# One resource for two engines in a planner, K of two heads in one load, a new order for the shared query tile, and norm rows in spare bank columns

## The chip, the cores and the metric

The kernel runs on one core of a Trainium2 chip. The metric is device time in microseconds. The kernel before took 733.95 us, the median of 3 runs (733.51 to 734.59). The execution that was profiled took 733.62 us, and its trace has a span of 731.5 us, so 2.1 us lie outside the span.

## The reference

Three blocks follow one another. Attention over 2 batches and 8 heads has pooled queries: neighbouring queries are averaged, so that 1152 keys meet 576 queries in each head. An MLP with softplus takes 512 features to 2048 and back. An RMS norm and a gated MLP with SiLU (512 to 1536 and back) end the work.

```python
# q, k, v: (2, 8, 1152, 64)
q_pool = q.reshape(B, H, S // 2, 2, D).mean(axis=3)
scores = scale * np.matmul(q_pool, k.transpose(0, 1, 3, 2))
scores = scores - np.max(scores, axis=-1, keepdims=True)
attn = np.exp(scores)
attn = attn / (np.sum(attn, axis=-1, keepdims=True) + 1e-09)
x = (attn @ v) reshaped to (1152, 512)
h = x @ w_in                                   # 512 -> 2048
g = np.maximum(h, 0.0) + np.log1p(np.exp(-np.abs(h)))
x = g @ w_out                                  # 2048 -> 512
rms = np.sqrt(np.mean(x * x, axis=-1, keepdims=True) + 1e-06)
xn = x / rms * rms_g
g = xn @ w_gate                                # 512 -> 1536
val = xn @ w_val
out = (g * sigmoid(g) * val) @ w_out           # 1536 -> 512
```

## The kernel before

**Numbers in two halves.** A float32 operand is kept as a high half, which the matmul format holds exactly, and a low half, the rest. A product is three matmuls: high by high, low by high, high by low (`terms`, L517 to L519). So each operand costs a cast (high) and a subtraction (low): `kk` for the keys, `qh` and `ql` for the queries, `gh` and `gl` for the hidden layer, `x` for the MLP inputs, `w` for the weights. The weights come packed and are first decoded by four operations (L296 on ACT, L301, L304 and L306 on DVE).

**Attention** goes over 8 pairs of heads. `prep` (L330) loads K, Q and V of a pair, adds neighbouring queries (`qs`), and makes the halves. `qk` (L378) makes a tile's scores for 128 queries of a head against all 1152 keys, in three banks `s`. `softmax` takes the maximum (`nm`, DVE, L407) and the exponential (`p`, ACT, L409). `flip` (L417) transposes `p` through two banks `t` and copies it to `pt`. `av` (L436) multiplies by V into a bank `t`, and a copy takes it to `O`. Each head has 4 whole query tiles; the two half tiles that are left are merged into a fifth, x = NF, the shared tile. There `scales` (L453) makes the factors of the row sums: `den` (L457), a reciprocal (L459), and two spreading copies `rdb` (L460, L463). The transposes of the shared tile are groups T[0], T[1], T[2] (`flip_m`, L655).

**The two MLPs** go over three blocks of 384 tokens. For each block, `project` makes hidden columns in the banks `s`, a softplus or SiLU on ACT follows (`g`, L539 or L630), `halve` makes `gh` and `gl`, and the second matrix accumulates in other banks. Between the MLPs, `norm_sum`, `norm_rows` (L582) and `norm` (L603) make the RMS norm of a block while the next block is projected. The sums of squares are turned into rows in a bank of the ring `banks["h"]`, the ring that `project` uses, read by DVE (L590), and the factors are transposed in that same bank and copied to `rs`.

**What sets the order.** All operations are recorded in a `Plan`. Its `run()` is a list scheduler: each operation has one or several engines with a cost each (`dve`, `act`, `pool`, L188 to L197) and a latest start; the operation that can start first goes first, ties by latest start. If another engine than the quickest is nearly as soon (within SLACK), it is preferred: POOL first, then ACT. The matmuls keep their recorded order. The instructions are then emitted by planned start, and on the chip each engine works through its own queue in that order.

**Names in the rows.** L248 is the helper `tt` (subtractions and sums on DVE or POOL), L243 is a copy or cast on ACT, L245 one on DVE, and L251 is a load. Buffer numbers after a name, as in `kk_2124`, tell pairs and rounds apart.

Of the kernel before, what the change touches and what calls it, by code (L numbers as in the profile page):

```python
# [12 lines left out]
F32 = mybir.dt.float32  # L13
# [48 lines left out]
class Plan:  # L62
# [40 lines left out]
    def order(self):  # L103
# [27 lines left out]
        for o in reversed(topo):  # L131
            e, d = o.opts[0]
# [12 lines left out]
    def run(self):  # L145
        free = dict.fromkeys(("PE", "ACT", "DVE", "POOL", "SP", "NONE"), 0.0)
# [7 lines left out]
        while ready:  # L154
            starts = [(max(free[e], o.ready), o, e, d) for o in ready for e, d in o.opts]
            low = min(x[0] for x in starts)
            t, o, e, d = min((x for x in starts if x[0] <= low + 1e-9), key=lambda x: (x[1].late, x[0] + x[3], x[1].n))
            found = [(t, e, d)]
            for x in starts:
                if x[1] is o and x[2] != e and not any(  # L160
                        y[2] == x[2] and y[1].late < o.late and y[0] < x[0] + x[3] for y in starts):
                    found.append((x[0], x[2], x[3]))
            t, e, d = min(found, key=lambda x: x[0] + x[2])
            for want in ("POOL", "ACT"):
                for t2, e2, d2 in found:
# [22 lines left out]
def dve(n, fast=False):  # L188
    return "DVE", 0.157 + n / (1920 if fast else 960)
# [11 lines left out]
def body(ctx: ExitStack, tc: tile.TileContext, kT, qT, v, w1, w1o, wg, wv, w2o, rg, outT):  # L201
# [48 lines left out]
    def load(out, src, kb, w):  # L250
        return op([("SP", 0.07 + kb / 220)], lambda e: nc.sync.dma_start(out=out(), in_=src), w=w, lat=2.2)  # L251
# [31 lines left out]
    def decode(n):  # L283
# [17 lines left out]
        op([("DVE", 0.6)], lambda e: nc.vector.tensor_scalar(out=t1(), in0=word(0), scalar1=29, scalar2=None,  # L301
# [28 lines left out]
    def prep(pb):  # L330
# [3 lines left out]
        s["q"] = qx[pb % 2]  # L334
        for h in range(2):
            spare = pb == 0 and h == 1
            qr = ring("a", "p1", [P, 2, SQ], F32, 2) if spare else ring("e", "qr", [P, 2, SQ])
            for z in range(2):
                load(lambda qr=qr, z=z: qr()[z * D:z * D + D], qT[n + h], 288, [(qr, z)])
            kr = ring("a", "p0", [P, S], F32, 2) if spare else ring("e", "kr", [P, S])  # L340
            for z in range(2):
                load(lambda kr=kr, z=z: kr()[z * D:z * D + D], kT[n + h], 288, [(kr, z)])
            qs = ring("e", "qs", [P, SQ])
            qh, ql = s["q"][h]
            op([pool(SQ)] if pb else [dve(SQ)], lambda e, qs=qs, qr=qr: tt(e, qs(), qr()[:, 0, :], qr()[:, 1, :], ALU.add),
# [3 lines left out]
            for x, m, src in ((0, f, 0), (c, D, f)):  # L349
# [51 lines left out]
    def softmax(pb, x, h):  # L401
# [5 lines left out]
        op([dve(S)], lambda e: nc.vector.tensor_reduce(out=nm(), in_=sc()[:, :, :N], axis=AX.XY, op=ALU.max, negate=True),  # L407
# [9 lines left out]
    def flip(pb, x, todo):  # L417
# [14 lines left out]
        op([act(n * P, False), dve(n * P)],  # L432
# [3 lines left out]
    def av(pb, x):  # L436
# [14 lines left out]
        op([dve(n), act(n, False)], lambda e: copy(e, o()[:, x * P:x * P + n], t()[:, :n]), r=[(t, None)], w=[(o, x)])  # L451

    def scales(pb):  # L453
# [353 lines left out]
```

## Time and profile before

| | |
|---|---|
| median of 3 runs | 733.95 us (733.51 to 734.59) |
| profiled execution | 733.62 us, its span 731.5 us |
| PE busy | 688.9 us, 94% of the span |
| DVE busy | 472.0 us, 65% |
| ACT busy | 305.7 us, 42% |
| POOL busy | 176.6 us, 24% |
| HBM read and written | 59.25 MB and 2.36 MB |

PE is the TensorE matmul queue, DVE the vector engine, ACT the scalar engine, POOL the GpSimd engine, SP the engine that issues most loads. A row of instructions gives start, duration, engine, line, operation, the tile written and the tile read. What stands in brackets is the time for which the engine sat idle before it, and what ended that idle time. The granted clock (PEclk) is a share of TensorE's full speed. In the 40 slices of the span, PE is below nine tenths in the first slice, in three others (at 8) and in the last (at 7).

### The profile page before, as it was taken

How to read it: one execution, taken by the hardware profiler on the slowest of the kernel's cores; microseconds unless marked ns; L12 is line 12 of the kernel's file. 1: busy time of each engine (PE TensorE's matmuls, PEld its weight loads, DVE VectorE, ACT ScalarE, POOL GpSimd, SP SyncE). 2: the span in 40 equal slices, each digit the busy share in tenths (PEclk: the TensorE clock that was granted, in tenths of full speed). 3: DMA queues.
4: the chain of work that ended last, by engine and by line, in shares of the span. 5: the costliest groups of instructions: out<-in, count | busy, mean ns of one | idle time of the engine just before them, and what ended most of it. 6: DMA issues, size and time to landing. Idle time of an engine off the chain costs nothing.

```text
span 731.5 us, 12416 instructions
## 1 busy us (share of the span) xinstructions
PE 688.9 (94%) x5083; PEld 660.4 (90%) x5083; DVE 472.0 (65%) x761; ACT 305.7 (42%) x549; POOL 176.6 (24%) x129
## 2 busy tenths in 40 slices
PE   2999999999989999999999999889999999999997
PEld 2889898888989889998999999879999999999997
DVE  5788988989886678997325368997974242222222
ACT  1766677777667674443211243434432111010001
POOL 0441634444330112320013134563440020000000
PEclk9999999999999999999999999989999999999999
DMA  9575538274410013444000014333440100000001
GB/s 218 141 187 132 151 94 208 76 187 112 138 42 26 1 59 116 161 157 143 1 1 1 30 58 144 129 132 115 151 138 30 43 1 1 1 26 19 0 1 44
DMA packets 19145, 62.41 MB, mean 85 GB/s; under 512 B 2704, under 2 KB 4240, under 8 KB 19088
## 3 DMA queue, kind: packets, MB, share of 16 engines
q1 hardware_dynamic: 18944, 61.61, 29.2%
q8 instruction: 40, 0.66, 0.4%
q14 instruction: 17, 0.14, 0.1%
q10 hardware_dynamic: 144, 0.00, 0.0%
HBM read 59.25 MB, written 2.36 MB: 84 GB/s over the span
## 4 chain that ended last, share of the span: by engine, by line
PE 72%; DVE 21%; issue 3%; ACT 2%; DMA 1%; SPq 0%; POOL 0%; DVEq 0%; ACTq 0%
PE s L517 11%; PE s L518 11%; PE s L519 11%; PE s L391 10%; PE t L446 9%; PE t L428 8%; PE t L517 4%; PE t L519 4%; PE t L518 4%; DVE t L306 3%; DVE t L304 3%; DVE nm L407 2%; DVE t L301 2%; DVE den L457 2%; DVE gh L245 1%
## 5 line engine op out<-in xcount | busy, mean ns | idle before, releaser
L517 PE MATMUL s<-x,w 128*128 128x384 f32 x348 | 118.5, 341 | 7.3 <-ACT g L539 3.0
L519 PE MATMUL s<-x,w 128*128 128x384 f32 x348 | 117.2, 337 | 0.0
L518 PE MATMUL s<-x,w 128*128 128x384 f32 x348 | 117.0, 336 | 0.0
L407 DVE TENSOR_REDUCE nm<-s 128x1 f32<-128x1152 f32 x72 | 97.0, 1354 | 27.9 <-PE s L391 24.9
L248 POOL TENSOR_TENSOR w<-t,w 128x512 fp32r<-128x512 f32 x54 | 75.6, 1402 | 144.9 <-ACT w L243 119.2
L409 ACT ACTIVATE p<-s,nm 128x1152 f32<-128x1152 f32 x72 | 88.1, 1223 | 20.5 <-DVE nm L407 18.7
L243 ACT COPY pt<-t 128x512 f32<-128x512 f32 (+1 forms) x130 | 68.5, 536 | 61.8 <-PE t L428 46.1
L428 PE MATMUL t<-ident,p 128*128 128x128 f32 x576 | 83.3, 278 | 9.2 <-DVE O L245 7.9
L517 PE MATMUL s<-gh,w 128*128 128x384 f32 x243 | 82.6, 340 | 2.7 <-DVE gh L245 2.7
L428 PEld LDWEIGHTS t<-ident,p 128*128 128x128 f32 x576 | 65.9, 141 | 19.2 <-ACT p L409 10.2
L518 PE MATMUL s<-gl,w 128*128 128x384 f32 x243 | 82.5, 339 | 0.6 <-DVE gl L248 0.6
L519 PE MATMUL s<-gh,w 128*128 128x384 f32 x243 | 82.2, 338 | 0.0
L446 PE MATMUL t<-pt,v 128*64 128x128 f32 (+1 forms) x1440 | 80.1, 265 | 2.1 <-ACT pt L243 2.1
L630 ACT ACTIVATE g<-s 128x384 f32<-128x384 f32 x36 | 17.7, 491 | 150.0 <-PE s L519 150.0
L446 PEld LDWEIGHTS t<-pt,v 128*64 128x64 f32 x1440 | 71.3, 137 | 9.3 <-issue 5.2
L517 PEld LDWEIGHTS s<-x,w 128*128 128x128 f32 x348 | 65.5, 188 | 10.0 <-ACT g L539 4.3
L245 DVE CAST gh<-g 128x384 fp32r<-128x384 f32 x75 | 36.3, 484 | 46.2 <-PE t L519 44.1
L518 PEld LDWEIGHTS s<-x,w 128*128 128x128 f32 x348 | 65.7, 189 | 0.0
L519 PEld LDWEIGHTS s<-x,w 128*128 128x128 f32 x348 | 65.6, 189 | 0.0
L296 ACT ACTIVATE t<-raw 128x512 f32<-128x512 f32 x68 | 45.7, 673 | 41.2 <-POOL w L248 24.8
L248 POOL TENSOR_TENSOR kk<-kr,kk 64x1152 fp32r<-64x1152 f32 x14 | 38.0, 2715 | 89.7 <-DVE kk L245 44.4
L306 DVE SCALAR_TENSOR_TENSOR t<-t,t 128x512 int32<-128x512 int32 x68 | 54.5, 801 | 3.6 <-ACT t L296 1.6
(135 smaller groups left out, 1211.1 us busy)
## 6 DMA issues: line engine op xcount, KB each, us to landing
kr<-in_kT_dram SPq DMA_DIRECT2D x30, 288.0 KB, 4.7
qr<-in_qT_dram SPq DMA_DIRECT2D x30, 288.0 KB, 6.1
raw<-in_w_dram SPq DMA_DIRECT2D x16, 512.0 KB, 3.7
raw<-in_w1o_dram SPq DMA_DIRECT2D x16, 512.0 KB, 3.6
raw<-in_wg_dram SPq DMA_DIRECT2D x12, 512.0 KB, 3.4
raw<-in_wv_dram SPq DMA_DIRECT2D x12, 512.0 KB, 3.4
raw<-in_w2o_dram SPq DMA_DIRECT2D x12, 512.0 KB, 3.4
v<-in_v_dram SPq DMA_DIRECT2D x16, 288.0 KB, 3.2
```

Source lines behind the costliest of these rows:

```text
L243: nc.scalar.copy(out, in_)
L248: engines[e].tensor_tensor(out=out, in0=in0, in1=in1, op=o)
L296: o = op([("ACT", 0.68)], lambda e: nc.scalar.activation(out=t0(), in_=word(1).bitcast(F32), scale=2.0 ** -112, **(dict(func=AF.Prelu, alp ...
L306: op([dve(DM)], lambda e: nc.vector.scalar_tensor_tensor(out=t0().bitcast(I32), in0=t0().bitcast(I32), scalar=3, in1=t1(), op0=ALU.logical ...
L391: nc.tensor.matmul(sc()[:, c, :N], lhsT=q, rhs=s["kk"][hh]()[:, c * N:(c + 1) * N], start=(hh == heads[0] and z == 0), stop=(hh == heads[- ...
L407: op([dve(S)], lambda e: nc.vector.tensor_reduce(out=nm(), in_=sc()[:, :, :N], axis=AX.XY, op=ALU.max, negate=True), r=[(sc, None)], w=[(n ...
L409: o = op([("ACT", 1.42)], lambda e: nc.scalar.activation(out=pr(), in_=sc()[:, :, :N], func=AF.Exp, bias=nm(), accum_out=s["den"]()[:, col ...
L428: nc.tensor.transpose(t()[:, i * P:(i + 1) * P], pr[:, c * P:(c + 1) * P], ident)
L446: nc.tensor.matmul(t()[h * D:h * D + D, :n], lhsT=s["v"][h]()[:, c, :], rhs=rhs, start=(c == 0), stop=(c == CK - 1))
L517: nc.tensor.matmul(out, lhsT=w[:, 0, cols], rhs=hi, start=start, stop=False)
L518: nc.tensor.matmul(out, lhsT=w[:, 0, cols], rhs=lo, start=False, stop=False)
L519: nc.tensor.matmul(out, lhsT=w[:, 1, cols], rhs=hi, start=False, stop=stop)
```

## The change

The change has four parts.

1. **Planner.** Every POOL operation, and every DVE operation that touches no PSUM bank, now also takes a common resource, "PORT": two of these never overlap in the plan. DVE operations that read PSUM are marked `psum=True` and stay free of it. POOL is not preferred any more; ACT still is, over DVE. A load costs the plan at least 0.6 us. The sums `qs` and the subtractions for `kk` may go to DVE or POOL.
2. **K of two heads in one load.** K of a pair is loaded once, as 128 partitions (64 for each head), where before each head's K was loaded twice into 64 partitions. Its high half is cast in place, its low half is written to the other 64 partitions. The Q loads of the first pair are issued from ACT's queue instead of SP's.
3. **Shared tile.** Its order was: scores of the next pair's first tile, T[0], T[1], `av` of the tile before, T[2]. Now it is T[0], T[1], the scores, T[2], `av`.
4. **Norm rows.** They are made in columns 384 to 511 of the three banks of the first ring entry, which `project` doesn't use, instead of in a bank of the ring.

The core of the diff:

```diff
-            starts = [(max(free[e], o.ready), o, e, d) for o in ready for e, d in o.opts]
+            starts = []
+            for o in ready:
+                for e, d, *port in o.opts:
+                    t = max(free[e], o.ready)
+                    if port or e == "POOL":
+                        t = max(t, free["PORT"])
+                    starts.append((t, o, e, d, bool(port) or e == "POOL"))
...
-            t, e, d = min(found, key=lambda x: x[0] + x[2])
-            for want in ("POOL", "ACT"):
-                for t2, e2, d2 in found:
-                    if e2 == want and e not in ("POOL", want) and t2 < t + SLACK and t2 + d2 + SLACK < o.late + self.span:
-                        t, e, d = t2, e2, d2
+            t, e, d, port = min(found, key=lambda x: x[0] + x[2])
+            for x in found:
+                if x[1] == "ACT" and e == "DVE" and x[0] < t + SLACK and x[0] + x[2] + SLACK < o.late + self.span:
+                    t, e, d, port = x
...
             free[e] = t + d
+            if port:
+                free["PORT"] = t + d
...
-def dve(n, fast=False):
-    return "DVE", 0.157 + n / (1920 if fast else 960)
+def dve(n, fast=False, psum=False):
+    t = 0.157 + n / (1920 if fast else 960)
+    return ("DVE", t) if psum else ("DVE", t, 1)
...
+        kr = ring("e", "kr", [P, S])
+        load(kr, kT[n:n + 2].rearrange("a d s -> (a d) s"), 576, [(kr, None)])
...
-                load(lambda qr=qr, z=z: qr()[z * D:z * D + D], qT[n + h], 288, [(qr, z)])
-            kr = ring("a", "p0", [P, S], F32, 2) if spare else ring("e", "kr", [P, S])
-            for z in range(2):
-                load(lambda kr=kr, z=z: kr()[z * D:z * D + D], kT[n + h], 288, [(kr, z)])
+                load(lambda qr=qr, z=z: qr()[z * D:z * D + D], qT[n + h], 288, [(qr, z)], "ACTQ" if pb == 0 else "SP")
...
-            op([pool(SQ)] if pb else [dve(SQ)], lambda e, qs=qs, qr=qr: tt(e, qs(), qr()[:, 0, :], qr()[:, 1, :], ALU.add),
+            op([dve(SQ), pool(SQ)], lambda e, qs=qs, qr=qr: tt(e, qs(), qr()[:, 0, :], qr()[:, 1, :], ALU.add),
...
+            hi, lo = slice(h * D, h * D + D), slice(D - h * D, P - h * D)
+            op([act(S)] if pb == 0 else [dve(S, True), act(S)], lambda e, kk=kk, hi=hi: copy(e, kk()[hi], kr()[hi]),
+               r=[(kr, None)], w=[(kk, 0)])
+            op([dve(S), pool(S)], lambda e, kk=kk, hi=hi, lo=lo: tt(e, kk()[lo], kr()[hi], kk()[hi], ALU.subtract),
+               r=[(kr, None), (kk, 0)], w=[(kk, 1)])
...
-    def norm_rows(t, acc, bank):
-        b, m, view = bank
+    def norm_rows(t, acc):
+        b, m, view = spare(0)
...
+    def spare(m):
+        sx = banks["h"][0][0]
+        if m == 0 and "spare" not in banks:
+            banks["spare"] = [plan.buf(lambda: sx()[:, :, N:]) for _ in range(2)]
+        return banks["spare"][m], None, lambda: sx()[:, m, N:]
...
                 scales(pb)
+                T[0]()
+                T[1]()
                 if not last:
                     qk(pb + 1, 0, 0)
-                T[0]()
-                if last:
+                else:
                     make_banks(1, "h")
                     m1_h(0)
-                T[1]()
+                T[2]()
                 av(*prev)
-                T[2]()
```

The planner's new resource changes which engine takes what. From before to after, the instructions on POOL that subtract `w` go from 54 to 21 (on DVE from 11 to 44), those that subtract `gl` from 9 to 0 (on DVE from 75 to 84), and those that make `x` of 384 columns from 20 to 12 (8 more on DVE). Casts go from DVE to ACT: `kk`, 15 on DVE to 5 and 1 on ACT to 11; `qh` of 512 columns, 15 to 2 and 1 to 14; `gh`, 75 to 66 and 9 to 18; `w`, 18 to 9 and 47 to 56.

DVE's queue at the first pair, before: `kk` is K in halves, `qs` the summed queries, `p_110` and `p_116` a lent buffer with K and Q of the second head, `nm` the maximum of the first scores.

```order
L245 CAST kk_108<-kr 128x1152
L248 TENSOR_TENSOR kk_108<-kr,kk_108 64x1152
L248 TENSOR_TENSOR qs<-qr 128x576
L374 TENSOR_SCALAR qhA_88<-qs 128x512
L355 SCALAR_TENSOR_TENSOR qlA_90<-qs,qhA_88 128x512
L355 SCALAR_TENSOR_TENSOR qlA_90<-qs,qhA_88 128x64
L245 CAST kk_130<-p_110 128x1152
L248 TENSOR_TENSOR kk_130<-p_110,kk_130 64x1152
L407 TENSOR_REDUCE nm_137<-s 128x1
L248 TENSOR_TENSOR qs<-p_116 128x576
L374 TENSOR_SCALAR qhB_92<-qs 128x512
L355 SCALAR_TENSOR_TENSOR qlB_94<-qs,qhB_92 128x512
```

The same stretch of DVE's queue after:

```order
L256 TENSOR_TENSOR qs<-qr 128x576
L383 TENSOR_SCALAR qhA_90<-qs 128x512
L363 SCALAR_TENSOR_TENSOR qlA_92<-qs,qhA_90 128x512
L256 TENSOR_TENSOR kk_114<-kr,kk_114 64x1152
L363 SCALAR_TENSOR_TENSOR qlA_92<-qs,qhA_90 128x64
L256 TENSOR_TENSOR qs<-p_107 128x576
L256 TENSOR_TENSOR kk_121<-kr,kk_121 64x1152
L416 TENSOR_REDUCE nm_142<-s 128x1
L363 SCALAR_TENSOR_TENSOR qlB_96<-qs,qhB_94 128x512
```

The casts of `kk` have left DVE for ACT, and the first subtraction of `kk` now stands behind the queries' halves.

DVE's queue where the fifth pair ends and the sixth begins, before (the shared tile's `den` and `rdb`, then the two first maxima of the next pair):

```order
L245 CAST kk_2124<-kr 128x1152
L374 TENSOR_SCALAR qhA_88<-qs 128x64
L355 SCALAR_TENSOR_TENSOR qlA_90<-qs,qhA_88 128x64
L245 COPY O<-t 128x128
L457 TENSOR_SCALAR den<-den 128x9
L459 RECIPROCAL den<-den 128x9
L245 COPY pt<-t 128x4x128
L460 COPY rdb<-den 128x512
L407 TENSOR_REDUCE nm_2169<-s 128x1
L407 TENSOR_REDUCE nm_2181<-s 128x1
L463 COPY rdb<-den 128x128
```

The same place after:

```order
L253 CAST kk_2067<-kr 64x1152
L363 SCALAR_TENSOR_TENSOR qlA_92<-qs,qhA_90 128x64
L253 COPY O<-t 128x128
L466 TENSOR_SCALAR den<-den 128x9
L468 RECIPROCAL den<-den 128x9
L469 COPY rdb<-den 128x512
L416 TENSOR_REDUCE nm_2110<-s 128x1
L416 TENSOR_REDUCE nm_2134<-s 128x1
L472 COPY rdb<-den 128x128
```

The row `L245 COPY pt` has left the place between the reciprocal and `rdb`; the rest stands as before.

POOL's queue at that place, before:

```order
L248 TENSOR_TENSOR x_765<-y,x_765 128x384
L248 TENSOR_TENSOR x_770<-y,x_770 128x192
L248 TENSOR_TENSOR kk_2124<-kr,kk_2124 64x1152
L248 TENSOR_TENSOR qs<-qr 128x576
L248 TENSOR_TENSOR w_2157<-t_2062,w_2157 128x512
```

And after:

```order
L256 TENSOR_TENSOR x_759<-y,x_759 128x384
L256 TENSOR_TENSOR x_761<-y,x_761 128x192
L256 TENSOR_TENSOR qs<-qr 128x576
L256 TENSOR_TENSOR kk_2067<-kr,kk_2067 64x1152
L256 TENSOR_TENSOR kk_2161<-kr,kk_2161 64x1152
L256 TENSOR_TENSOR w_2179<-t_1827,w_2179 128x512
```

The sum `qs` now stands ahead of `kk`, and two subtractions of `kk` stand together.

## Rows read from the trace of the kernel before

**Rows 1.** The page: busy time of each engine.

```profile
PE 688.9 (94%) x5083; PEld 660.4 (90%) x5083; DVE 472.0 (65%) x761; ACT 305.7 (42%) x549; POOL 176.6 (24%) x129
```

**Rows 2.** PE's groups by line and shape: busy, mean ns, idle before, releasers.

```profile
L517 PE MATMUL s<-x,w 128*128 128x384 f32 x348 | 118.5, 341 | 7.3 <-ACT g L539 3.0 <-DVE n L590 2.6 <-ACT g L630 0.6
...
L428 PE MATMUL t<-ident,p 128*128 128x128 f32 x576 | 83.3, 278 | 9.2 <-DVE O L245 7.9 <-ACT p L409 0.9 <-ACT pt L243 0.2
L517 PE MATMUL s<-gh,w 128*128 128x384 f32 x243 | 82.6, 340 | 2.7 <-DVE gh L245 2.7
L518 PE MATMUL s<-gl,w 128*128 128x384 f32 x243 | 82.5, 339 | 0.6 <-DVE gl L248 0.6
...
L517 PE MATMUL t<-x,w 128*128 128x384 f32 x108 | 36.8, 340 | 2.0 <-ACT rs L243 1.3 <-DVE rs L245 0.7
```

**Rows 3.** Stretches of the span: busy time and count by engine, granted clock, DMA, GB/s.

```profile
84.00:240.00 156.00, 149.23 (x1567) 135.44 (x1566) 127.11 (x192) 111.44 (x195) 56.60 (x36) 1.00 0.42 111
430.00:490.00 60.00, 53.50 (x297) 51.74 (x296) 55.50 (x75) 26.42 (x48) 32.29 (x24) 0.97 0.38 126
486.80:493.30 6.50, 5.87 (x17) 5.47 (x18) 6.38 (x8) 2.85 (x4) 3.65 (x3) 0.50 0.45 153
541.00:544.50 3.50, 3.50 (x13) 3.49 (x12) 1.74 (x2) 1.10 (x3) 2.41 (x3) 0.51 0.75 240
600.00:640.00 40.00, 40.00 (x232) 40.00 (x232) 8.84 (x18) 2.95 (x6) 0.00 (x0) 1.00 0.00 1
```

**Rows 4.** The timeline, DVE at the longest wait of the decode stage.

```profile
485.35 1.44 DVE L245 CAST gh<-g 128x384 fp32r<-128x384 f32 x1
```

**Rows 5.** The timeline where the fifth pair of heads ends.

```profile
172.53 2.66 POOL L248 TENSOR_TENSOR kk<-kr,kk 64x1152 fp32r<-64x1152 f32 x1 [6.71 <-DVE qhA L374]
...
173.05 2.18 DVE L457 TENSOR_SCALAR den<-den 128x9 f32<-128x9 f32 x1
...
175.27 1.42 POOL L248 TENSOR_TENSOR qs<-qr 128x576 f32<-128x576 f32 x1
...
175.94 1.04 DVE L460 COPY rdb<-den 128x512 f32<-128x512 f32 x1
...
176.90 2.61 DVE L407 TENSOR_REDUCE nm<-s 128x1 f32<-128x1152 f32 x2
...
177.46 2.19 PE L446 MATMUL t<-pt,v 128*64 128x128 f32 x36 [0.29 <-ACT pt L243]
...
179.54 1.22 ACT L409 ACTIVATE p<-s,nm 128x1152 f32<-128x1152 f32 x1
...
181.15 0.63 PE L428 MATMUL t<-ident,p 128*128 128x128 f32 x4 [1.24 <-DVE O L245]
```

**Rows 6.** One tile's instructions, `den`: durations least, median and most, in ns.

```profile
L457 DVE TENSOR_SCALAR den<-den x8: 173/2174/2304, 41.7 to 270.9; 128x9 f32<-128x9 f32 x8
...
L460 DVE COPY rdb<-den x8: 416/1038/1466, 44.7 to 274.0; 128x512 f32<-128x512 f32 x8
```

**Rows 7.** The timeline where the sixth pair ends, PE.

```profile
214.30 0.63 PE L428 MATMUL t<-ident,p 128*128 128x128 f32 x4 [1.70 <-DVE O L245]
```

**Rows 8.** The timeline of the start.

```profile
8.43 0.76 DVE L248 TENSOR_TENSOR qs<-qr 128x576 f32<-128x576 f32 x1 [0.42 <-DMA qr<-in_qT_dram]
...
16.95 1.16 PE L391 MATMUL s<-kk,qlB 128*128 128x384 f32 x3
```

**Rows 9.** Two stretches of the start, columns as above.

```profile
2.00:6.00 4.00, 0.00 (x0) 0.00 (x0) 0.20 (x2) 0.01 (x1) 0.00 (x0) 1.00 1.02 237
12.00:15.80 3.80, 0.00 (x0) 0.00 (x0) 3.67 (x4) 1.24 (x3) 0.00 (x0) 1.00 1.06 287
```

**Rows 10.** Groups of DVE and ACT by line and shape: prices.

```profile
L248 DVE TENSOR_TENSOR w<-t,w 128x512 fp32r<-128x512 f32 x11 | 7.5, 686 | 0.3 <-ACT w L243 0.2
```

**Rows 11.** The same view for ACT.

```profile
L243 ACT CAST w<-t 128x512 fp32r<-128x512 f32 x47 | 29.0, 621 | 29.1 <-DVE t L306 27.6 <-PE t L518 1.4
...
L243 ACT CAST kk<-kr 128x1152 fp32r<-128x1152 f32 x1 | 1.1, 1141 | 0.0
```

More of the change, by code (lines that the diff above doesn't have):

```diff
@@ L131, in order @@
         for o in reversed(topo):
-            e, d = o.opts[0]
+            e, d = o.opts[0][:2]
             need = 0.0
@@ L145, in run @@
     def run(self):
-        free = dict.fromkeys(("PE", "ACT", "DVE", "POOL", "SP", "NONE"), 0.0)
+        free = dict.fromkeys(("PE", "ACT", "DVE", "POOL", "SP", "ACTQ", "PORT", "NONE"), 0.0)
         self.free = free
@@ L154, in run @@
         while ready:
-            starts = [(max(free[e], o.ready), o, e, d) for o in ready for e, d in o.opts]
+            starts = []
[5 more added lines that the diff above has]
+                    starts.append((t, o, e, d, bool(port) or e == "POOL"))
             low = min(x[0] for x in starts)
-            t, o, e, d = min((x for x in starts if x[0] <= low + 1e-9), key=lambda x: (x[1].late, x[0] + x[3], x[1].n))
-            found = [(t, e, d)]
+            t, o, e, d, port = min((x for x in starts if x[0] <= low + 1e-9), key=lambda x: (x[1].late, x[0] + x[3], x[1].n))
+            found = [(t, e, d, port)]
             for x in starts:
@@ L171, in run @@
                 fits = [x for x in starts if x[2] == e and x[0] + x[3] <= u[0] + 1e-9 and len(x[1].opts) == 1]
-                t, o, e, d = min(fits, key=lambda x: (x[0], x[1].late, x[1].n)) if fits else u
+                t, o, e, d, port = min(fits, key=lambda x: (x[0], x[1].late, x[1].n)) if fits else u
             ready.remove(o)
@@ L248, in tt, with load @@
         engines[e].tensor_tensor(out=out, in0=in0, in1=in1, op=o)
-    def load(out, src, kb, w):
-        return op([("SP", 0.07 + kb / 220)], lambda e: nc.sync.dma_start(out=out(), in_=src), w=w, lat=2.2)
+    def load(out, src, kb, w, queue="SP"):
+        q = nc.sync if queue == "SP" else nc.scalar
+        return op([(queue, 0.6 + max(0, kb / 220 - 0.6))], lambda e: q.dma_start(out=out(), in_=src), w=w, lat=2.2)
     xs = [fixed("k", f"x{t}", [P, 2 * KC * N], F32R) for t in range(NBLK)]
@@ L456, in scales @@
         rd = s["rd"] = ring("a", "rdb", [P, NF + 1, 2, D])
-        op([("DVE", 0.17)], lambda e: nc.vector.tensor_scalar(out=den(), in0=den(), scalar1=1e-9, scalar2=None, op0=ALU.add),
+        op([("DVE", 0.17, 1)], lambda e: nc.vector.tensor_scalar(out=den(), in0=den(), scalar1=1e-9, scalar2=None, op0=ALU.add),
            w=[(den, None)])
-        op([("DVE", 0.25)], lambda e: nc.vector.reciprocal(den(), den()), w=[(den, None)])
+        op([("DVE", 0.25, 1)], lambda e: nc.vector.reciprocal(den(), den()), w=[(den, None)])
         op([dve(NF * P)], lambda e: nc.vector.tensor_copy(
```

54 lines of the change are left out of this document (26 added, 28 removed).

## The prediction

> **What bounds the kernel now.** I read the page's busy times first, then PE's groups by line, then single stretches and the timeline at PE's longest waits. PE is busy for 688.9 of 731.5 us [rows 1], so what can be won lies in its waits and in stretches at a low clock. PE's groups name the waits [rows 2]: at the pair boundaries the transposes wait 7.9 us for DVE's copy of `O`; the projections wait 3.0 for ACT's softplus `g` and 2.6 for the norm's DVE row L590; the second matrices of the MLP wait 2.0 for `rs`; and the hidden layer's products wait 2.7 for `gh` and 0.6 for `gl`. Two stretches hold a granted clock near one half, so the lower level of 1.2 GHz: 486.8 to 493.3 and 541.0 to 544.5 [rows 3]. The first stands right behind the 2.7 us wait for `gh` (one wait: the group's only one), the second behind a wait of the norm. In attention DVE works 127 of 156 us and ACT 111 [rows 3]; in the decode stage DVE works 55.5 of 60 us, which is why the `gh` wait exists.
>
> DVE is slower than it needs to be. `den`, 9 columns, takes 0.17 us at best and 2.17 in the median; `rdb` takes 0.42 at best and 1.04 in the median [rows 6]. The long ones lie under a POOL instruction: `den` starts at 173.05 while POOL works on `kk` from 172.53 to 175.19, and ends 0.04 us behind it; `rdb` starts at 175.94 under POOL's `qs` [rows 5]. A cast of `gh` takes 1.44 us in the decode stage [rows 4]. In the same stretch at the boundary the maxima, which read PSUM, run at 1.31 us each, under POOL work or not. This is what the planner's new resource describes.
>
> **The change part by part**, against the profiled 733.62 us; that lies 0.33 below the median of 733.95, within the runs' spread.
>
> *Norm rows.* The next projection no longer shares a bank with the norm's rows and transposes, so its waits for L590 and, through the same ring, those of the second matrix for `rs` have no cause left: 2.6 + 2.0 = −4.6. What comes next in PE's queue has its operands long before, since the projection reads `x` and weights only. A new wait could be that the next norm's rows wait for the `rs` copy of the last one, but that lies a whole block back. With the wait before 541 gone, I take its low clock to go too. A steady stretch has 232 matmuls in 40.0 us, 0.172 each; the 13 of the slow stretch would take 2.24 in place of 3.50 [rows 3]: −1.3.
>
> *Planner, decode stage.* 33 subtractions of `w`, 9 of `gl` and 8 of `x` move from POOL to DVE. On DVE one of `w` costs 0.69 [rows 10], so 33 × 0.69 = 23 us of DVE work are added over the whole kernel; against that nothing holds DVE up where POOL is empty, and 9 casts of `gh` and 9 of `w` leave for ACT, which has room (26 of 60 us busy [rows 3]). Which of the two sums is larger can't be read off the order. A `gh` that costs 1.44 where nothing else but a cast of 384 columns is done shows a DVE that loses about 1 us each time; from the busy stretch I take it that the queue gets shorter. Then the waits for `gh` and `gl` go, 2.7 + 0.6 = −3.3, and the clock stays up behind them: 17 matmuls, 5.87 us busy, at 0.172 would take 2.93: −2.9. Of ACT's `g` waits I take half, 3.0 / 2 = −1.5, since ACT gets 18 more casts there at about 0.6 [rows 11] and loses waits on DVE. Bounds for this part: nothing gained (0) to all of it gained (−9.2, with the whole 3.0); I take −7.7.
>
> *Shared tile and POOL's order at the boundary.* The transposes of the next tile don't wait for the copy of `O` any more, as `av` is recorded behind T[2]. What is late next is ACT's exponential. PE's flip at 181.15 needs the exponential that starts at 179.54 and takes 1.22 [rows 5], so it ends at 180.76, and some 0.2 later with its sum: hardly before the flip started. And the chain ahead of it moves. POOL now has `qs`, then `kk`, back to back: 1.42 + 2.66 = 4.08 us. If the first starts about where POOL's `kk` starts before, 172.5 to 172.8, that is up to 174.2 and on to 176.9. `den` stands under `qs` and comes out at 174.2; the reciprocal isn't held; `rdb` starts under `kk` and comes out at 177.2, where before it ended at 176.98. The two maxima stand behind it, 2 × 1.31, to 179.85; the exponential and its sum end at 181.4; the flip starts near 181.65, half a us later. PE's scores of that tile come about 1.1 later too, since T[0] and T[1] stand ahead of them, but this is hidden under the wait of the maxima for `rdb`. For the five boundaries that look alike this is 5 × 0.5 = +2.5; the first and the last I take at 0. If `rdb` isn't held, the maxima start near 177.3 with their scores, the flip near 180.5, and each boundary is worth −0.65: that is a rival below, and the bounds are −3.3 and +5 (both subtractions of `kk` that stand together in POOL's queue fall under it).
>
> *K in one load, and the start.* Of SP's K loads 34 become 8; the bytes halve. In the middle the loads are hidden, and the gain is nothing. At the start the first score tiles wait for them: the sum `qs` starts at 8.43 when the first Q lands, and the second head's first scores end at 18.11 [rows 8]. After, DVE's order from Q's landing L is `qs` 0.76, `qhA` 0.43, `qlA` 0.69, the subtraction of `kk` 1.36 (its cast is on ACT, done before): scores start at L + 3.3 and end at L + 5.8. Then `qs` and `kk` of the second head, the maximum at L + 5.8 to 7.1, `qlB` to L + 7.9, the second scores end at L + 9.0. With L unchanged at 8.43 that is 17.4: −0.7. L itself hangs on the loads. Ahead of the first Q's end 1.15 MB move in either program. The loads that go to 64 partitions run at 237 GB/s, those mixed with V, which goes to 128, at 287 [rows 9]: at 287 they take 4.0 in place of 4.9 us, L is 7.5; at 237 with a share of V squeezed in between, as Q now comes from a queue of its own, 8.8. So the second scores end at 16.5 to 17.8, −1.6 to −0.3; I take −0.7, L unchanged. The Trainium skill, page "SBUF — State Buffer", section "Can I just issue two DMAs to hit both halves?", says that two transfers to two halves of the partitions serialize, and that only one over all 128 reaches every port; by it the K load gets faster and the sum at the start would be −1.6. Against the second queue speaks "DMA: Bandwidth & Descriptors", section "Issuing engines are not separate DMA queues": loads issued by several engines interleave on the same 16 DMA engines, and only the issue time is saved; by it Q and K land together, later than the first Q did, and it would be −0.3. The two rates above fit the first, the trace of before has no load on a second queue to test the second.
>
> *Casts on ACT.* In attention ACT gains 11 casts of `kk` at 1.14 and 13 of `qh` at 0.62 [rows 11], 12.5 + 8.1 = 20.6 us. ACT works 111 of 156 us there [rows 3], so there is room, but an exponential behind a cast is late by the cast. What hides them: PE scores and transposes other tiles while ACT casts. Bounds 0 to +20.6; I take +1.0, near the low end, as the row on ACT shows 45 us idle in 156, and DVE loses as many casts.
>
> The sum: −4.6 − 1.3 − 3.3 − 2.9 − 1.5 + 2.5 − 0.7 + 1.0 = −10.8, so 733.6 − 10.8 = **722.8 us**.
>
> **Rivals.**
>
> *A: the boundaries get shorter.* POOL's `kk` starts earlier or later than DVE's `rdb`, and the boundary gives 5 × 0.65 = 3.3 back in place of costing 2.5: 717.0. For it: the planner keeps the two apart on paper. Against it: nothing in the order holds POOL's `kk` back from the moment at which `qs` ends.
>
> *B: the decode stage stays bound by DVE*, and the change doesn't do there what it says. The new resource is a plan; on the chip POOL and DVE still run when their inputs are there, and 50 more instructions stand in a queue that was busy 55.5 of 60 us. Then the −7.7 fail: 730.5. For it, that row; against it, that so much of those 55.5 us is waiting under POOL.
>
> *C: slower, by the clock.* The waits at the five boundaries grow from 1.24 to about 1.75. A wait of 1.70 at the sixth pair's end [rows 7] was not followed by a low clock, as the stretch around it has 1.00 [rows 3]; one of the norm's, shorter than 2.6, was. If each of the five is followed by a drop that costs 2.9, as the one behind `gh` did, that is +14.7: 737.5. It decides from 4 drops, 10.8 / 2.9. Against it: the transposes and scores around a boundary did not drop at 1.70.
>
> *D: slower, by ACT.* The casts stand in front of exponentials on which PE waits. If three quarters of 20.6 us, 15.5, came on the path in place of 1.0, the time is 737.3; it decides from 11.8 us. For it: ACT's share rises from 71% of the stretch; against it: 45 us idle there.
>
> **How the numbers follow.** 0.2% of the time, about 1.5 us, is what can be told from no change: 732.5 to 735.4. My forecast has 0.55, A 0.15, B 0.20, C 0.05, D 0.05. The forecast is faster but for 0.03 (0.02 the same, 0.01 slower); A is faster; of B 0.15 is faster, 0.035 the same, 0.015 slower; C and D are slower. So faster 0.82, same 0.055, slower 0.125, rounded to 0.82, 0.06 and 0.12. The range reaches from below A, 715, to just above B, 731; outside stay C, D, a tenth of B and the best end of A.
>
> **What would show it.** In the new profile: no wait of PE for L590's successor or for `rs`; no low clock around 541; one around 487 only if `gh` still waits (then B). At the boundaries the flip's wait is put down to ACT's `p`, about 1.7 us each, with `rdb` near 1.5 us or longer under POOL's `kk` (if it takes 0.42, it is A). `qs` of the first pair starts between 7.5 and 8.8, and the second scores end near 17.4. ACT's `g` waits stand near 1.5. The prediction is wrong if DVE's busy share in the decode stage doesn't fall below 55 of 60 us, or if PE waits for `p` within pairs, not at their ends.

## The result and the profile after

The changed kernel took 716.4 us (median of 4 runs, 715.7 to 717.6) against 733.9 for the kernel before. The ratio is 0.976, with a 95% interval of 0.975 to 0.978: 17.5 us faster, where 10.8 were forecast. The profiled execution has a span of 714.2 us, and its granted clock is full as long as PE works.

PE's timeline divides the gain. First the kernel before, the first four of attention's last five transposes, and the last matmul (start, duration):

```profile
281.51 0.65 PE L479 MATMUL t<-ident,rdb 128*128 128x128 f32 x4
...
726.55 0.34 PE L519 MATMUL t<-gh,x 128*128 128x384 f32 x1
```

Then the kernel after:

```profile
281.50 0.66 PE L488 MATMUL t<-ident,rdb 128*128 128x128 f32 x4
...
709.28 0.34 PE L528 MATMUL t<-gh,x 128*128 128x384 f32 x1
```

Attention ends at the same time in both. All of the gain lies in the MLPs and the norm, which take 17.3 us less. Their waits are gone from PE's groups (busy, mean ns, idle before, releasers; they answer to [rows 2]):

```profile
L526 PE MATMUL s<-x,w 128*128 128x384 f32 x348 | 117.8, 338 | 1.3 <-ACT g L647 0.6 <-ACT rs L251 0.6
...
L437 PE MATMUL t<-ident,p 128*128 128x128 f32 x576 | 82.7, 277 | 11.0 <-ACT p L418 10.8 <-ACT pt L251 0.2
L526 PE MATMUL s<-gh,w 128*128 128x384 f32 x243 | 81.5, 335 | 0.0
...
L527 PE MATMUL s<-gl,w 128*128 128x384 f32 x243 | 81.4, 335 | 0.0
...
L526 PE MATMUL t<-x,w 128*128 128x384 f32 x108 | 36.3, 336 | 0.0
```

The waits for the softplus `g`, `gh`, `gl` and L590 stand at nothing; of `rs` the third remains. In the place of 7.9 us of waiting for `O`, the flips now wait 10.8 us for the exponential.

The stretches of [rows 3], after, with the start's stretches of [rows 9] behind them (PE, PEld, DVE, ACT, POOL busy, clock, DMA share, GB/s):

```profile
84.00:240.00 156.00, 148.59 (x1564) 134.99 (x1563) 120.64 (x164) 118.85 (x215) 51.39 (x34) 1.00 0.29 88
430.00:490.00 60.00, 59.42 (x346) 58.93 (x344) 47.82 (x92) 28.71 (x53) 4.14 (x3) 1.00 0.37 123
...
2.00:6.00 4.00, 0.00 (x0) 0.00 (x0) 0.06 (x1) 0.98 (x2) 0.00 (x0) 1.00 0.91 290
6.00:10.40 4.40, 0.00 (x0) 0.00 (x0) 0.00 (x0) 1.33 (x2) 0.00 (x0) 1.00 1.04 209
```

In the decode stage DVE does 92 instructions in 47.8 us, where before it did 75 in 55.5: 17 more, in less time, with POOL busy for 4.1 us in place of 32.3. The groups of DVE say the same of single operations:

```profile
L256 DVE TENSOR_TENSOR w<-t,w 128x512 fp32r<-128x512 f32 x44 | 30.0, 685 | 4.9 <-ACT w L251 4.9
L253 DVE CAST gh<-g 128x384 fp32r<-128x384 f32 x66 | 26.0, 394 | 43.9 <-PE t L528 41.7 <-ACT g L548 1.2
```

The 44 subtractions of `w` keep the price of [rows 10], and a cast of `gh` takes 394 ns on average. The 1.44 us of [rows 4] was one under POOL, as this row of the kernel before shows:

```profile
485.30 1.27 POOL L248 TENSOR_TENSOR w<-t,w 128x512 fp32r<-128x512 f32 x1 [2.01 <-ACT w L243]
```

The boundary of [rows 5], after:

```profile
173.13 1.42 POOL L256 TENSOR_TENSOR qs<-qr 128x576 f32<-128x576 f32 x1 [7.29 <-PE t L455]
...
173.37 1.21 DVE L466 TENSOR_SCALAR den<-den 128x9 f32<-128x9 f32 x1
...
174.63 2.66 POOL L256 TENSOR_TENSOR kk<-kr,kk 64x1152 fp32r<-64x1152 f32 x1
...
174.86 2.71 DVE L469 COPY rdb<-den 128x512 f32<-128x512 f32 x1
...
177.49 2.61 DVE L416 TENSOR_REDUCE nm<-s 128x1 f32<-128x1152 f32 x2
...
180.23 1.23 ACT L418 ACTIVATE p<-s,nm 128x1152 f32<-128x1152 f32 x1
...
181.60 0.66 PE L437 MATMUL t<-ident,p 128*128 128x128 f32 x4 [1.78 <-ACT p L418]
```

`den` under `qs`, `rdb` under `kk`, the maxima behind it, the flip at 181.60: the chain came as worked out (174.2, 177.2, 179.85, 181.65), within 0.4 us at each step. That the flip is right to 0.05 is in part luck: POOL's `qs` began 0.3 later than assumed, and the steps behind the maxima took 0.3 less.

The start, which answers to [rows 8]:

```profile
10.49 0.76 DVE L256 TENSOR_TENSOR qs<-qr 128x576 f32<-128x576 f32 x1 [8.43 <-DMA qr<-in_qT_dram]
...
18.34 0.79 PE L400 MATMUL s<-kk,qlB 128*128 128x384 f32 x3 [0.75 <-DVE qlB L363]
```

The first Q landed 2.06 us later than before, outside the bounds of 7.5 to 8.8; the second scores end at 19.13. From that landing on the chain held: L + 9.0 would be 19.5.

### The profile page after: what moved, and what is told of

It reads as the page before. It is cut to its first block, busy times and chain, and to the rows that moved or that the text cites. A ratio compares the mean times of both kernels' runs of the same rounds, so it can differ in the third digit from the quotient of the medians.

```text
span 714.2 us, 12314 instructions
## 1 busy us (share of the span) xinstructions
PE 681.2 (95%) x5083; PEld 654.8 (92%) x5083; DVE 447.5 (63%) x755; ACT 334.6 (47%) x609; POOL 100.2 (14%) x75
## 4 chain that ended last, share of the span: by engine, by line
PE 88%; DVE 6%; ACT 4%; DMA 1%; issue 1%; ACTq 0%; DVEq 0%
PE s L526 15%; PE s L528 15%; PE s L527 15%; PE s L400 10%; PE t L455 9%; PE t L437 9%; PE t L528 5%; PE t L527 5%; PE t L526 5%; ACT p L418 2%; DVE rdb L469 2%; DVE nm L416 1%; DMA qr<-in_qT_dram 1%; PE t L488 1%; DVE den L466 1%
## 5 line engine op out<-in xcount | busy, mean ns | idle before, releaser
L418 ACT ACTIVATE p<-s,nm 128x1152 f32<-128x1152 f32 x72 | 88.1, 1224 | 21.7 <-DVE nm L416 19.7
L437 PE MATMUL t<-ident,p 128*128 128x128 f32 x576 | 82.7, 277 | 11.0 <-ACT p L418 10.8
L251 ACT COPY pt<-t 128x512 f32<-128x512 f32 (+2 forms) x138 | 70.4, 521 | 35.9 <-PE t L437 28.9
L526 PE MATMUL s<-gh,w 128*128 128x384 f32 x243 | 81.5, 335 | 0.0
L528 PE MATMUL s<-gh,w 128*128 128x384 f32 x243 | 81.5, 335 | 0.0
L305 ACT ACTIVATE t<-raw 128x512 f32<-128x512 f32 x68 | 45.1, 671 | 21.0 <-DVE w L256 13.4
L256 DVE TENSOR_TENSOR gl<-g,gh 128x384 fp32r<-128x384 f32 x84 | 48.4, 577 | 9.3 <-ACT gh L251 7.1
L253 DVE CAST gh<-g 128x384 fp32r<-128x384 f32 x66 | 26.0, 394 | 43.9 <-PE t L528 41.7
L649 DVE TENSOR_TENSOR g<-g,s 128x384 f32<-128x384 f32 x18 | 9.9, 552 | 62.5 <-ACT g L647 59.3
L315 DVE SCALAR_TENSOR_TENSOR t<-t,t 128x512 int32<-128x512 int32 x68 | 48.0, 705 | 1.7
```

What stands on the lines that cost most here:

```text
L251: nc.scalar.copy(out, in_)
L256: engines[e].tensor_tensor(out=out, in0=in0, in1=in1, op=o)
L305: o = op([("ACT", 0.68)], lambda e: nc.scalar.activation(out=t0(), in_=word(1).bitcast(F32), scale=2.0 ** -112, **(dict(func=AF.Prelu, alp ...
L315: op([dve(DM)], lambda e: nc.vector.scalar_tensor_tensor(out=t0().bitcast(I32), in0=t0().bitcast(I32), scalar=3, in1=t1(), op0=ALU.logical ...
L418: o = op([("ACT", 1.42)], lambda e: nc.scalar.activation(out=pr(), in_=sc()[:, :, :N], func=AF.Exp, bias=nm(), accum_out=s["den"]()[:, col ...
L437: nc.tensor.transpose(t()[:, i * P:(i + 1) * P], pr[:, c * P:(c + 1) * P], ident)
```

## The experiments

"Us" is the median, and the ratio is to the kernel before as measured beside each run, where its median was between 733.8 and 734.6 us; a difference between two runs of well under 1 us is not to be read. "Attention" is where its last product with V ends (the last transposes end 0.7 to 1.0 us behind it), "rest" is from there to the last matmul's end, both from PE's timeline of the profiled execution.

| run | us | ratio, 95% interval | attention | rest |
|---|---|---|---|---|
| before | 733.9 | | 281.6 | 445.3 |
| the change | 716.4 | 0.976 (0.975 to 0.978) | 281.6 | 428.0 |
| norm alone | 730.7 | 0.995 (0.994 to 0.997) | 282.0 | 441.9 |
| planner alone | 719.0 | 0.979 (0.978 to 0.981) | 276.5 | 437.1 |
| old planner, DVE alone | 720.8 | 0.982 (0.980 to 0.983) | 282.2 | 432.8 |
| change without the resource | 736.6 | 1.004 (1.003 to 1.005) | 292.7 | 436.6 |
| planner + norm | 714.1 | 0.972 (0.971 to 0.974) | 276.3 | 431.6 |
| planner + norm + tile | 711.1 | 0.968 (0.967 to 0.970) | 276.1 | 428.8 |
| change, old tile order | 718.7 | 0.979 (0.977 to 0.980) | 284.3 | 428.0 |
| change, Q on SP | 714.1 | 0.972 (0.971 to 0.974) | 279.8 | 428.1 |
| change, POOL as before | 713.4 | 0.971 (0.970 to 0.973) | 278.9 | 428.1 |
| the two edits above | 710.0 | 0.967 (0.966 to 0.969) | 275.8 | 428.0 |
| change, rdb on ACT | 712.4 | 0.971 (0.970 to 0.973) | 278.1 | 428.0 |
| tile alone | 743.8 | 1.014 (1.012 to 1.016) | 294.1 | 445.9 |

**Norm alone.** The kernel before with part 4:

```diff
-            norm_rows(t - 1, acc[t - 1], banks["h"][(i + 3) % 4])
+            norm_rows(t - 1, acc[t - 1])
...
-            norm(t - 1, acc[t - 1], banks["h"][(i + 3) % 4])
+            norm(t - 1, acc[t - 1])
```

> The kernel before, with the norm's rows and transposes alone moved to spare bank columns. Theory (the bank was the cause): PE's waits for L590 (2.6 us) and for rs (2.0) and the low clock behind 541 go, with what PE loses around them; in the trace of before these places cost 3.6 + 2.1 us over a steady pace, so about -6, 728. Rival (DVE's lag was the cause, and the wait only moves): the waits for g, gh and gl grow by what is won, 732 or more.

Measured: −3.4 us, between the two theories. L590's wait is gone and `rs` falls to 1.4, but PE's waits (us in total, times, longest) show a new one, 4.5 us for DVE's product `g`:

```profile
PE s L517 <- DVE g L640: 4.5, 2, 4.2
PE s L517 <- ACT g L539: 2.9, 4, 1.6
PE t L446 <- ACT pt L243: 2.1, 7, 0.3
PE s L517 <- ACT rs L243: 1.4, 2, 0.8
```

The bank was the cause of the old waits; but DVE, late as it is under the old planner, collects part of the gain in a wait further on.

**Planner alone.** The kernel before with part 1, but without that part's price for a load and its free choice between DVE and POOL for `qs` and `kk`; everything else as before:

```diff
+                    if port or e == "POOL":
+                        t = max(t, free["PORT"])
...
-            for want in ("POOL", "ACT"):
...
-    return "DVE", 0.157 + n / (1920 if fast else 960)
+    t = 0.157 + n / (1920 if fast else 960)
+    return ("DVE", t) if psum else ("DVE", t, 1)
```

> The kernel before, with the planner alone changed (one resource for POOL and for DVE without PSUM, POOL not preferred); loads, shared tile and norm as before. Theory: PE's waits for g (3.0), gh (2.7) and gl (0.6) go and the low clock behind 487 with them; these places cost 4.2 + 6.5 us over a steady pace, so -9 to -11, 723 to 725; the norm's waits stay near 4.6. Rival (a plan holds nothing back on the chip, DVE stays the bound): 731 or more.

Measured: −15.1, more than the theory said. In the profiled execution, which is one of the run's two slower ones (720.1, the others 717.4 to 720.2), the rest gains 8.2, and attention 5.1, which no step of the prediction had. The view of `den` shows why (least, median, most in ns; [rows 6] is its counterpart):

```profile
L465 DVE TENSOR_SCALAR den<-den x8: 161/164/264, 47.0 to 273.6; 128x9 f32<-128x9 f32 x8
...
L468 DVE COPY rdb<-den x8: 415/428/429, 47.5 to 274.8; 128x512 f32<-128x512 f32 x8
```

Under this plan only one `den` of eight, the one of 264 ns, starts while POOL works, and no `rdb` does; the maxima stand ahead of them in DVE's queue, and the flips wait 0.2 us in place of 1.24.

**Old planner, DVE alone.** The kernel before, with POOL struck out as a choice for the late `w`, for `gl`, for `x` and for the norm's sums; its work on the first `w`, on `qs` and on `kk` stays:

```diff
-        op([pool(DM)] if n < EARLY else [dve(DM), pool(DM)], lambda e: tt(e, view()[:, 1, :], t0(), view()[:, 0, :], ALU.subtract),
+        op([pool(DM)] if n < EARLY else [dve(DM)], lambda e: tt(e, view()[:, 1, :], t0(), view()[:, 0, :], ALU.subtract),
...
-        op([dve(N), pool(N)], lambda e: tt(e, gl(), g(), gh(), ALU.subtract), r=[(g, None), (gh, None)], w=[(gl, None)])
+        op([dve(N)], lambda e: tt(e, gl(), g(), gh(), ALU.subtract), r=[(g, None), (gh, None)], w=[(gl, None)])
...
```

> The kernel before with its old planner, but the subtractions of late w, of gl, and of x, and the norm's sums, allowed on DVE alone. Theory (what counts is that POOL does not run beside DVE in the decode stage, not the accounting): the same 723 to 726 as with the new planner. Rival (DVE is overloaded by 44 more subtractions, and the accounting picks the few that POOL can take free of charge): no gain or slower, 733 to 740.

Measured: −13.4, some 2 us better than the theory's range, all of it in the rest (432.8). The decode stage:

```profile
430.00:490.00 60.00, 58.51 (x338) 57.83 (x337) 46.07 (x91) 26.03 (x49) 1.10 (x1) 1.00 0.36 116
```

DVE's 91 instructions take 46.1 us with POOL at 1.1. So the theory holds for that stage: what counts is that POOL is still there, and a plan without the resource can have that too. Attention keeps its 282, since its POOL work was not touched. Whether the whole change would do as well with POOL struck out in place of the resource was not run.

**Change without the resource.**

```diff
-                    if port or e == "POOL":
-                        t = max(t, free["PORT"])
```

> The changed kernel without the common resource in the plan: POOL still not preferred, all else as changed. POOL gets 39 subtractions of w (21 with the resource) and 7 of gl (0). Theory (what counts is who gets the work): between, 719 to 724, with a wait for gh or g back in the decode stage. Rival (not preferring POOL was the whole gain): 716 to 717.

Measured: 736.6, slower than the kernel before, and outside what either theory gave. Attention ends 11.1 us later than in the change, and the rest is 8.6 longer, with a wait of 4.2 us for DVE's product `g`, as the theory had it. At its boundaries `den` stands under a `kk` of POOL's again, and PE's transposes of the shared tile wait for a copy `pt` that stands behind `den` in DVE's queue:

```profile
181.95 2.65 POOL L254 TENSOR_TENSOR kk<-kr,kk 64x1152 fp32r<-64x1152 f32 x1 [6.87 <-DVE kk L251]
...
182.35 2.28 DVE L464 TENSOR_SCALAR den<-den 128x9 f32<-128x9 f32 x1
...
184.68 1.40 POOL L254 TENSOR_TENSOR qs<-qr 128x576 f32<-128x576 f32 x1
184.79 0.63 DVE L251 COPY pt<-t 128x512 f32<-128x512 f32 x1
185.34 1.02 DVE L467 COPY rdb<-den 128x512 f32<-128x512 f32 x1
185.48 1.09 PE L679 MATMUL t<-ident,p 128*128 128x128 f32 x8 [1.07 <-DVE pt L251]
```

**Planner and norm; and the tile on top.** The kernel before with part 1 as in "planner alone" and part 4, then with part 3 too (diffs as above and in the change).

> The kernel before with the planner's new resource and the norm's spare columns, without the K load and without the new order of the shared tile. Theory: the two add up where the planner alone still waits for the norm (0.7 + 0.7 + 3.2 us over a steady pace), so 719.0 - 4.7 = 714, faster than the whole change at 716.4, as the planner alone ended attention at 276.5 against 281.6. Rival (the wait moves on, as it moved to g of the gated MLP with the norm alone): 718 to 719.

> As the run before, with the new order of the shared tile added; K still loaded for each head. Theory (the new K part is what sets den and rdb ahead of the maxima and under POOL): within 1.5 us of the run without it, 713 to 716. Rival (the shared tile's order alone makes the flip wait for the exponential, 1.78 in place of 0.23 at six boundaries): +6 or more, 720.

Measured: 714.1, as the theory said to 0.2 us: with DVE on time, the norm's part is worth 4.9. With the tile 711.1: another −3.0, below the theory's range, and faster than the whole change by 5.3. The rival falls: the shared tile's order isn't what delays the flips. Nor does its gain lie at the pair boundaries: attention ends only 0.2 earlier, the rest is 2.8 shorter, and of PE's waits there those for `gl` in the 35 us behind attention (2.0 us in three) are gone. What the change has beyond this run is part 2 (K in one load, Q from ACT's queue) and the rest of part 1 (the price for a load, the free choice for `qs` and `kk`). These together, "the K part" in what follows, cost the change 5.3 us.

**Change with the old tile order.**

```diff
+                if not last:
+                    qk(pb + 1, 0, 0)
                 T[0]()
...
                 T[1]()
-                if not last:
-                    qk(pb + 1, 0, 0)
...
-                T[2]()
                 av(*prev)
+                T[2]()
```

> The changed kernel with the shared tile in its old order. Theory (K part): rdb still stands ahead of the maxima and under POOL's kk, so nothing is won, 715 to 718. Rival (the shared tile's order is the cause): attention ends near 276.5 again, so 711.

Measured: 718.7, 2.3 more than the change and a little above the theory's range: the new order is a gain here too, and the theory's rival falls. `rdb` is held as in the change (2.7 us in the median of eight).

**Change with Q on SP.**

```diff
-                load(lambda qr=qr, z=z: qr()[z * D:z * D + D], qT[n + h], 288, [(qr, z)], "ACTQ" if pb == 0 else "SP")
+                load(lambda qr=qr, z=z: qr()[z * D:z * D + D], qT[n + h], 288, [(qr, z)], "SP")
```

> The changed kernel with the first pair's Q loads back on SP's queue, behind K's one load and ahead of V's. Theory (Q from ACT's queue shares the DMA engines with K and V and lands late, at 10.49 in place of 8.43): qs starts near 8, the first scores come 2 to 2.5 us earlier, 714 to 714.5. Rival (the bytes are the limit, whichever queue they stand in): qs starts after 10, 716.

Measured: 714.1, −2.3, as the theory said, though not by its steps. The plan also sets both subtractions of `kk` ahead of the sum, which starts at 9.22, not near 8, and no longer waits for Q; the first scores come 3.3 us earlier (10.59 in place of 13.87), the second end 2.9 earlier:

```profile
9.22 0.76 DVE L256 TENSOR_TENSOR qs<-qr 128x576 f32<-128x576 f32 x1
...
14.90 1.33 PE L400 MATMUL s<-kk,qlB 128*128 128x384 f32 x3 [0.90 <-DVE qlB L363]
```

**Change with POOL's work in attention as before, and with Q on SP too.**

```diff
-            op([dve(SQ), pool(SQ)], lambda e, qs=qs, qr=qr: tt(e, qs(), qr()[:, 0, :], qr()[:, 1, :], ALU.add),
+            op([pool(SQ)] if pb else [dve(SQ)], lambda e, qs=qs, qr=qr: tt(e, qs(), qr()[:, 0, :], qr()[:, 1, :], ALU.add),
...
-            op([dve(S), pool(S)], lambda e, kk=kk, hi=hi, lo=lo: tt(e, kk()[lo], kr()[hi], kk()[hi], ALU.subtract),
+            op([pool(S)] if pb else [dve(S)], lambda e, kk=kk, hi=hi, lo=lo: tt(e, kk()[lo], kr()[hi], kk()[hi], ALU.subtract),
```

> The changed kernel, but from the second pair on the sums qs and the subtractions of kk are given to POOL alone, as before (in the change they may go to DVE or POOL). In DVE's queue the two maxima then stand ahead of den and rdb again. Theory (the free choice changes the due times, which set rdb ahead of the maxima, where POOL's kk holds it): the flips' waits fall from 1.7 to about 0.6 each, the start stays, 711 to 713. Rival (one load of K or the casts on ACT cost it): 715.5 to 717.

> As the run before, with the first pair's Q loads on SP's queue as well. Theory (the two causes add up): 2.3 less than the run before, 709 to 710, the best of all. Rival (they are one cause): 711 to 713.

Measured: 713.4 (−3.0) and 710.0. The first lies 0.4 over its range, with the cause as expected: the maxima stand ahead of `den` and `rdb` again, `rdb` takes 0.43, the flips wait 0.6:

```profile
PE t L437 <- ACT p L418: 4.1, 7, 0.6
```

The second is the fastest of all, 6.4 us under the change: −2.3 and −3.0 add up, with 1.1 over. So Q's queue and the free choice are the whole cost of the K part. What is left of that part, K in one load with its casts on ACT, can be read off 710.0 against the 711.1 of planner, norm and tile: about 1 us won at most, not clear of the scatter between runs.

**Change with rdb on ACT.**

```diff
-        op([dve(NF * P)], lambda e: nc.vector.tensor_copy(
-            rd()[:, :NF], den()[:, :2 * NF].rearrange("p (h x) -> p x h", h=2).unsqueeze(3).to_broadcast([P, NF, 2, D])),
+        op([act(NF * P)], lambda e: copy(
+            e, rd()[:, :NF], den()[:, :2 * NF].rearrange("p (h x) -> p x h", h=2).unsqueeze(3).to_broadcast([P, NF, 2, D])),
```

> The changed kernel with the long rdb copy (512 columns) given to ACT, which POOL cannot hold. Theory (the hold of rdb by POOL's kk is what delays the maxima behind it): the maxima start with their scores, the flips' waits fall by 0.6 to 1.1 at each of 6 boundaries, 710 to 713. Rival (the scores, which come about 1.1 later in the new order of the shared tile, are the limit): 716 to 717.

Measured: 712.4, −4.0. POOL's `kk` stands there as before, and ACT isn't held:

```profile
173.35 2.65 POOL L256 TENSOR_TENSOR kk<-kr,kk 64x1152 fp32r<-64x1152 f32 x1
173.64 0.62 ACT L251 COPY rdb<-den 128x512 f32<-128x512 f32 x1
...
173.97 1.36 DVE L416 TENSOR_REDUCE nm<-s 128x1 f32<-128x1152 f32 x1 [0.42 <-PE s L400]
...
179.12 0.66 PE L437 MATMUL t<-ident,p 128*128 128x128 f32 x4 [0.57 <-ACT p L418]
```

The maximum takes 1.36 under that same `kk`, as elsewhere; only the wait for `rdb` had kept it back. That settles the hold as the cause of the flips' 1.78.

The boundaries gain more than the totals of this run and of "POOL as before" show. From one pair's transposes of `rdb` to the next's, the five pairs behind the first take 164.9 us in the change, 160.5 with POOL as before and 158.9 with `rdb` on ACT: −4.4 and −6.1. The first pair is 1.7 and 2.4 us longer in these two profiled executions, in part because PE's first scores keep their slow pace for longer, as the third tile's show, first in the change, then with `rdb` on ACT:

```profile
19.43 0.77 PE L400 MATMUL s<-kk,qhA 128*128 128x384 f32 x3
```

```profile
20.01 1.31 PE L400 MATMUL s<-kk,qhA 128*128 128x384 f32 x3
```

The granted clock reads 1.00 there in both, and what ends the slow pace no run here shows.

**Tile alone.** The kernel before with part 3 only.

> The kernel before with the new order of the shared tile alone. Theory: the waits for O (7.9) and pt (2.1) go, waits for the exponential of about 1.2 take their place, as rdb is still held by POOL: -1 to -3, 731 to 733. Rival (the later scores make the exponential 1.1 later): +0 to +5, 734 to 739.

Measured: 743.8 (743.3 to 746.3; the execution that was profiled is the longest of them), +10.0, worse than the rival. Where the old planner put things, the copy of `pt` that frees a bank `t` for T[1] stands behind a `den` that POOL holds:

```profile
179.84 2.21 DVE L457 TENSOR_SCALAR den<-den 128x9 f32<-128x9 f32 x1
...
182.90 0.66 PE L664 MATMUL t<-ident,p 128*128 128x128 f32 x4 [1.02 <-DVE pt L245]
```

PE now meets that copy earlier, and waits 8.9 us for it over the 11 times that it does. In the profiled execution attention is 12.5 us longer. At its flips, transposes and products PE idles some 7 us more, and behind two of the six boundaries the granted clock falls as well:

```profile
148.00:151.60 3.60, 3.60 (x21) 3.16 (x21) 2.10 (x3) 2.06 (x4) 0.00 (x0) 0.53 0.97 221
219.60:223.20 3.60, 3.60 (x19) 3.16 (x21) 2.10 (x3) 2.06 (x4) 0.00 (x0) 0.53 0.93 253
```

By 3.6 × 0.47 that is an estimated 1.7 us each. The same edit is worth −3.0 on the new plan.

## Why the prediction was right, and where it was not

**Norm rows: right.** L590's and two of the three `rs` waits went, and the clock behind them stayed full. But only in company: alone they gave 3.4 of the 5.9 that were summed, with the new planner 4.9.

**Decode stage: right in its mechanism, too small.** Its rival falls (B): DVE took 17 more instructions and needed less time, and the run with DVE alone shows that POOL's absence is enough there. With the norm the forecast for the rest was −13.6, measured −17.3. Two sizes were off. Of the waits for `g` I took half; all 3.0 went. And a wait costs PE more than its idle time shows: at 332.5 before, a wait shown as 1.53 put the next matmul 1.86 behind the last, 1.69 more than the steady 0.172 of [rows 3]:

```profile
332.51 0.34 PE L519 MATMUL t<-gh,w 128*128 128x384 f32 x1
334.37 0.44 PE L517 MATMUL s<-x,w 128*128 128x384 f32 x1 [1.53 <-ACT g L539]
```

The first matmul behind it is slower as well (0.44). Nearly the whole rest, before and then after (columns of [rows 3]):

```profile
284.00:726.00 442.00, 429.41 (x2438) 425.39 (x2437) 244.77 (x409) 114.98 (x216) 86.23 (x66) 0.99 0.19 64
```

```profile
284.00:709.00 425.00, 423.19 (x2440) 421.15 (x2439) 228.73 (x441) 124.20 (x236) 19.39 (x16) 1.00 0.20 68
```

At 40.0 / 232 us for a matmul, 2438 take 420.3 and 2440 take 420.7: PE before was 21.7 us over the steady pace, after 4.3. Of these 17.4 I had counted 13.6, as idle rows and slow clock.

**Boundaries: the chain was right, its price was not.** The gap grew by 0.5 as forecast, but 0.29 of waiting for `pt` ahead of `av` went at each, 2.1 in all over seven, that I had left at nothing. So a pair costs 0.2 more in place of 0.5, and the first pair, from its first flip to its boundary's, is 1.4 shorter. Rival A, which did not come, is nearly what the planner alone does: there `rdb` takes 0.43. The free choice for `qs` and `kk` brought `rdb` ahead of the maxima again and under POOL, and took 3.0 us back (4.4 at the boundaries themselves). I had asked what the change does to the boundary as a whole; I had not asked what each part does to it alone.

**The start: wrong, in sign and in mechanism.** The step "With L unchanged at 8.43" failed, and the bounds with it. I let K's faster load make up for the second queue. K did land sooner (its first cast starts at 5.03, before at 5.86), but Q, from its own queue, ran beside K and V and landed at 10.49. The rule that I had weighed, "Issuing engines are not separate DMA queues" in the Trainium skill's page "DMA: Bandwidth & Descriptors", gave the direction in which L moved, not the size. By the price that I set on it, −0.3, I took Q to come later by a share of V at most. The run with Q on SP gives 2.3 us back, the new order in DVE's queue included. Between 2.0 and 10.4 us the queues moved 290 × 4.0 + 209 × 4.4 = 2080 KB, where K and the first Q, 128 × 1152 numbers of 4 bytes each, are 1180: some 900 of the 1180 KB of V and the second Q went ahead of the first Q's end.

**Casts on ACT: nearly free.** PE waits for the exponential within pairs only once, 0.76 us in the first. So +1.0 was too much, and rival D falls. **The clock (C):** five gaps of 1.7 to 1.8 in attention, and the clock stays full in every slice. The rival was not an idle one, as the run with the tile alone shows: two of its boundaries, with waits of 1.0 and 0.6, were followed by a clock of 0.53.

**The total.** The forecast missed by 6.7 us, and its two halves miss the same way: the rest gained 3.7 more than the 13.6 forecast, and attention, for which +2.5 − 0.7 + 1.0 = +2.8 was forecast, lost nothing. Inside attention the errors cancel: the start came 1.7 us worse than forecast, boundaries and casts better. That the time lies next to rival A's 717.0 is luck, as A's chain did not come.

## What to carry to other kernels

Where POOL and DVE share work, count POOL's time twice: once for itself and once for what it holds up on DVE, and let the planner know it: the planner alone gave 15.1 us here, and no POOL in the decode stage, without the planner's knowing, 13.4. A change of several parts is to be priced part by part: the same tile order cost 10.0 us on one plan and gave 3.0 on the other, and two details, a second queue and a free choice, took 5.3 us back unseen, because the total was good. Giving a planner more choices isn't free: a free choice for `qs` and `kk` set an unrelated pair of small instructions ahead of the maxima and onto the critical chain. By which step of the planner it did so (their due times, I take it) no run shows.

## What the runs showed of the hardware that was not expected

A DVE instruction on SBUF that comes up while POOL works lasted, in the rows above, to the end of POOL's instruction or up to 0.3 us beyond, whatever its own size: `den`, 9 columns, 0.16 us by itself, took up to 2.3 us, and `rdb` 2.71 beside 2.66 of POOL, while the maximum out of PSUM took 1.36 under such a `kk`.

A wait on PE is followed by a low clock in some places and not in others. Behind 4.2 us for `g` in the run with the norm alone the granted clock was 0.55 (near the lower level of 1.2 GHz), and in the run with DVE alone it was 0.59 behind a wait of only 1.03 that followed the norm's one-column matmuls:

```profile
526.62 0.80 PE L587 MATMUL s<-ones,ms 128*128 128x1 f32 x6 [0.30 <-DVE g L632]
528.45 0.44 PE L517 MATMUL s<-x,w 128*128 128x384 f32 x1 [1.03 <-DVE n L590]
```

The stretch behind it (PE busy, clock, DMA share, GB/s):

```profile
529.30:533.00 3.70, 3.70 (x15) 0.59 0.73 251
```

The five gaps of 1.7 to 1.8 in the change's attention had none. In the run with the tile alone waits of 1.02 and 0.61, with four transposes between them, were followed by 0.53 at two boundaries (148.0 and 219.6), and at another with the same two waits (182.9) by no drop.
